# Attention, MLP and token mixer on one core: transposes of two heads in one step, the leftover block one place earlier, a surcharge for POOL in the planner, and new intervals

## The chip, the cores and the metric

The kernel runs on one core of one Trainium2 chip. The metric is the device time of one execution in microseconds (us), the median of several runs. TensorE is called PE, VectorE DVE, ScalarE ACT, GpSimd POOL and SyncE SP; SP's queue issues the DMA transfers.

## The reference, cut to what matters

```
scores = q @ k.T / 8 + min(-(cum_i - cum_j), 0), causal      # B=4, H=8, S=576, D=64
x  = softmax(scores) @ v, heads joined                        # [4, 576, 512]
x  = x + relu(layernorm(x) * g @ w_ch1) @ w_ch2               # 512 -> 2048 -> 512
u  = x + ((x.T @ U) @ V).T                                    # token mixer, rank 32
out = u + relu(u @ w2_ch1) @ w2_ch2                           # second MLP, 512 -> 2048 -> 512
```

cum is the running sum of max(s, 0). All of it is float32; the kernel reaches that by splitting both factors of a product into a high and a low part and doing three matmuls for one.

## The kernel before

**Blocks.** Work is cut by batch and tokens: A (tokens 0 to 255) and B (256 to 575) of each batch go through attention, layernorm and the first MLP. Then C (tokens 0 to 511 of a batch) goes through mixer and second MLP, where mlp1 is done as seven products in place of eight; T0 is the 64 leftover tokens of all four batches as one block of 256 columns. GROUPS gives the order of the first layer's steps, LAST that of the second: C0, C1, C2, C3, T0.

**The planner.** Nothing is issued where it is written. Every operation is given to a class Plan with a priority, its modelled duration on each engine that could do it, and what it reads and writes. `plan()` simulates the engines, takes for each operation the engine on which it would end first (times a price for busy engines), and so finds an order; `latest()` turns an order into due times; `issue()` does this four times and issues the best order, each engine's instructions in their planned places. Each engine works its list off in order, so a late operand holds up all that stands behind it. The DMA loads, `load()`, stand in SP's list in the same manner. Bare matmuls on ones (L1593) fill planned idle time of PE ahead of the first MLP step.

**The tables.** AT says over which of the first layer's steps the attention of a block is spread, LN where its layernorm stands, HEAD by how many us due times of some priorities are shifted.

**Attention.** `score` puts a pair of heads' scores into PSUM (L765, L769) and DVE adds the bias and takes the row maximum (L752); ACT and POOL do exponent and normalization (L780 to L801). `trans` then transposes each head's weights on PE in blocks of 128 columns (L824, three or four blocks a head, one PE operation for each head), and the result is split into pB (L381 on ACT, L386 on DVE). PV is L895. The layernorm's last steps are L1009 and L1050.

**The MLPs.** L1386 to L1388 and L1443 to L1445 are the three matmuls each of the first and second linear layer for A, B and T; L1308 to L1310 and L1345 to L1347 those of C. DVE and ACT combine C's products (L1288, L1294, L1268, L1269), `mlp2c` holds the second layer of C, its add of the residual and its stores (L1356); T's add and stores are L1453 and L1457. A helper records every split: high part by ACT or DVE (L381, L382), low part by DVE or POOL (L386, L388).

Of the kernel before, what the change touches and what calls it, by code (L numbers as in the profile page):

```python
# [26 lines left out]
LAG = 2  # L27
# [1 line left out]
FULL = ("A0", "A1")  # L29

GROUPS = (("A0", "A1"), ("A2", "A3"), ("B0",), ("B1",), ("B2",), ("B3",))
LAST = ("C0", "C1", "C2", "C3", "T0")
W2SLOTS = 12

AT = {"A2": (1, 3), "A3": (1, 34), "B0": (26, 49), "B1": (50, 64), "B2": (69, 84), "B3": (80, 100)}
LN = {"A2": 9, "A3": 34, "B0": 62, "B1": 64, "B2": 85, "B3": 102}
W0 = (1, 14)
HEAD = {-100: -1, -50: 127, 1.5: 71, 4.5: 8, -4: 3, -3: 0}
W1 = (16, 60, 59)
PASSES = 4  # L40
AHEAD = 1500


def f(ap):
# [3 lines left out]
def mm_cost(n):  # L48
    return max(106.7, n / 2.4) + 13.3
# [39 lines left out]
class Plan:  # L89
# [63 lines left out]
    def plan(self, prio, price):  # L153
# [42 lines left out]
        while avail:  # L196
            best = {}
            tent = dict(free)
            avail.sort(key=lambda o: (prio[o.seq], o.seq))
            for o in avail:  # L200
                fin = None
                for e, (dur, _) in o.alts.items():
                    s = slot(o, e)
                    if s is None:
                        continue
                    s = max(s, o.ready[e], dma_free - BACKLOG if e == "sp" else 0.0)
                    port = e in o.port
                    f0 = max(s, tent.get(e, 0.0), tent.get("port", 0.0) if port else 0.0) + dur
                    if len(o.alts) > 1:
                        w = min(int(s / WIN), NW - 1)  # L210
                        f0 += (price[e][w] + (price["port"][w] if port else 0.0)) * dur + (o.soft if e == "dve" else 0.0)
                    if fin is None or f0 < fin[0]:
                        fin = (f0, max(s, free[e], free["port"] if port else 0.0), e, dur)
                if fin is None:
                    continue
                e = fin[2]
                for g in (e, "port") if e in o.port else (e,):
                    if fin[1] <= tent.get(g, 0.0):
                        tent[g] = tent.get(g, 0.0) + fin[3]
# [12 lines left out]
            if o.nbytes:
                o.end = dma_free = max(dma_free, s + 1100) + o.nbytes
            new = []
            for b in o.bufs:
                if not b.live:
                    lst = live[b.tag]
                    base, most = self.take.get(b.tag, (None, 0))
                    if len(lst) < cap[b.tag]:
                        b.slot = f"{b.tag}{len(lst)}"  # L240
                    else:
                        src = lst
                        if cap[b.tag] < most:
# [92 lines left out]
def mha_ffn_mixer_ffn(ctx: ExitStack, tc, qkv_p, qkv_a, qkv_b, s, g, w1, w2, U, V, out):  # L336
# [22 lines left out]
    def psum():  # L359
        return P.buf("ps", [128, 512])  # L360
# [9 lines left out]
    def pe(prio, cost, fn, reads, writes, hold=()):  # L370
        return P.op(prio, {"pe": (cost, fn)}, reads, writes, hold=hold)
# [245 lines left out]
    class Pair:  # L617
# [187 lines left out]
        def trans(self, prio, tick):  # L805
# [9 lines left out]
            else:  # L815
                groups = [(None, ts[0], [S - 128, 0, 128, 256]), (None, ts[0], [384])]
            first = 0
            for z, t, blocks in groups:
                ps = psum()
                n = len(blocks)  # L820

                def tr(ps=ps, t=t, blocks=blocks):
                    for j, c in enumerate(blocks):
                        nc.tensor.transpose(ps[:, 128 * j:128 * (j + 1)], t[:, c:c + 128], ident.tile)  # L824

                pe(prio - 500, n * 109, tr, [t, ident], [ps] + [(a, i) for a in pT])

                def view(a, z=z, n=n, first=first):
                    if self.blk == "A":
# [502 lines left out]
    def mlp2c(st, half):  # L1332
        _, b, _, m = steps[st]
        w, h = w2t[st], hbuf[st]
        ks = (0, 1) if half == 0 else (2, 3)
        run = runs[st]
        first, last = st == run["first"], st == run["last"]
        if first:
            run[half] = [P.buf("acc", [128, 512]), psum()]
        aa = run[half]  # L1340

        def mm():
            for z, k in enumerate(ks):
                sl = slice(128 * k, 128 * (k + 1))
                nc.tensor.matmul(aa[z].tile, w[:, 0, sl], h[:, 0], start=first, stop=False)  # L1345
                nc.tensor.matmul(aa[z].tile, w[:, 1, sl], h[:, 0], start=False, stop=False)  # L1346
                nc.tensor.matmul(aa[z].tile, w[:, 0, sl], h[:, 1], start=False, stop=last)  # L1347

        free2[st] = pe(st + LAG + 0.5, 6 * mm_cost(512), mm, [w, h], aa)
        if last:  # L1350
            x = xt[b, "C"][0][half]
            for z, a in enumerate(aa):
                kk = [(x, (z, y)) for y in range(2)]
                k = ks[z]
                dve(st - 1000, 512, lambda a=a, z=z: nc.vector.tensor_tensor(out=x[:, z], in0=x[:, z], in1=a.tile, op=ALU.add), [a] + kk, kk)
                load(st - 1000, 128 * 2048, lambda k=k, z=z: nc.sync.dma_start(out[128 * k:128 * (k + 1), b * S:b * S + 512], x[:, z]), kk, [])  # L1356
            if half == 1:
                xt.pop((b, "C"))
        if half == 1:
            del hbuf[st]  # L1360
# [282 lines left out]
```

## Time and profile before

| | |
|---|---|
| time, median of 3 runs | 1036.17 us (1035.99 to 1036.62) |
| the profiled execution's own time | 1035.96 us |
| its span, first to last instruction | 1034.1 us |
| mean granted TensorE clock | 0.998 |
| PE busy | 1016.1 us, 98% |
| DVE busy | 670.8 us, 65% |
| ACT busy | 491.1 us, 47% |
| POOL busy | 163.1 us, 16% |

A busy time is the sum of an engine's instructions over the span; the profiled time is 1.9 us longer than the span. Matmuls overlap in the records, so the distance from one start to the next is what a matmul costs in a row of them.

### The profile page before, as it was taken

What the parts mean: (1) busy time and instruction counts of PE and PEld (TensorE: products, weight loads), DVE (VectorE), ACT (ScalarE), POOL (GpSimd) and SP (SyncE); (2) the same over time, 40 slices, a digit from 0 to 9 for tenths busy, and PEclk for the clock granted to TensorE, in tenths of its full rate; (3) what the DMA queues carried; (4) which work ended last, traced back from release to release, by engine and by line L of the source; (5) the groups of instructions that cost most, each with busy time, mean ns of one, the idle gap of its engine ahead of it and who ended that gap; (6) DMA issues with size and microseconds to landing.
All of it is one profiled execution on the core that took longest, in us unless ns stands there. A gap on an engine that the chain in (4) does not pass through costs nothing.

```text
span 1034.1 us, 19346 instructions
## 1 busy us (share of the span) xinstructions
PE 1016.1 (98%) x7102; PEld 937.0 (91%) x7102; DVE 670.8 (65%) x1688; ACT 491.1 (47%) x1155; POOL 163.1 (16%) x305
## 2 busy tenths in 40 slices
PE   8999999999999999999999999999999999999997
PEld 6888979899999989998999999898999898889997
DVE  7988987976978567677754328547446645844521
ACT  8988877855867456666553214213111211211210
POOL 0011342330522213423210003001001000200000
PEclk9999999999999999999999999999999999999999
DMA  9999986389737886567457798991763574376383
GB/s 312 350 344 318 335 296 215 126 244 304 244 106 241 274 291 226 179 219 232 169 182 287 247 393 338 334 342 53 263 217 117 178 260 163 113 257 206 117 285 102
DMA packets 98078, 245.12 MB, mean 237 GB/s; under 512 B 16288, under 2 KB 46240, under 8 KB 93632
## 3 DMA queue, kind: packets, MB, share of 16 engines
q1 hardware_dynamic: 97888, 243.83, 68.5%
q8 instruction: 56, 0.92, 0.3%
q14 instruction: 38, 0.31, 0.1%
q10 hardware_dynamic: 96, 0.07, 0.0%
HBM read 190.30 MB, written 62.99 MB: 245 GB/s over the span
## 4 chain that ended last, share of the span: by engine, by line
PE 81%; DMA 8%; DVE 7%; ACT 2%; issue 1%; SPq 1%; DVEq 0%; ACTq 0%
PE ps L1386 6%; PE ps L1387 6%; PE ps L1388 6%; PE ps L1308 5%; PE ps L1310 5%; PE ps L1309 5%; PE ps L866 4%; PE ps L824 4%; PE acc L1443 4%; PE acc L1444 3%; PE acc L1445 3%; PE acc L1346 3%; PE acc L1345 3%; PE acc L1347 3%; PE ps L1345 3%; PE ps L1347 3%
## 5 line engine op out<-in xcount | busy, mean ns | idle before, releaser
L1386 PE MATMUL ps<-xh,w 128*128 128x256 f32 (+1 forms) x512 | 160.0, 312 | 0.7 <-DVE hl L1393 0.6
L1388 PE MATMUL ps<-xl,w 128*128 128x256 f32 (+1 forms) x512 | 151.9, 297 | 0.0
L1387 PE MATMUL ps<-xh,w 128*128 128x256 f32 (+1 forms) x512 | 151.8, 296 | 0.0
L1393 DVE SCALAR_TENSOR_TENSOR hl<-ps,hh 128x256 fp32r<-128x256 f32 (+1 forms) x144 | 64.8, 450 | 106.2 <-ACT hh L1392 105.5
L1392 ACT ACTIVATE hh<-ps 128x256 fp32r<-128x256 f32 (+1 forms) x144 | 58.2, 405 | 130.7 <-PE ps L1388 130.1
L1386 PEld LDWEIGHTS ps<-xh,w 128*128 128x128 f32 x512 | 97.2, 190 | 6.6 <-issue 1.9
L1387 PEld LDWEIGHTS ps<-xh,w 128*128 128x128 f32 x512 | 97.3, 190 | 2.0
L1443 PE MATMUL acc<-hh,w 128*128 128x256 f32 (+1 forms) x320 | 98.2, 307 | 0.0
L1388 PEld LDWEIGHTS ps<-xl,w 128*128 128x128 f32 x512 | 97.1, 190 | 0.0
L1268 ACT ACTIVATE w<-hl 128x256 fp32r<-128x256 f32 x91 | 37.1, 416 | 123.6 <-DVE hl L1288 123.5
L1444 PE MATMUL acc<-hh,w 128*128 128x256 f32 (+1 forms) x320 | 93.8, 293 | 0.0
L1445 PE MATMUL acc<-hl,w 128*128 128x256 f32 (+1 forms) x320 | 93.7, 293 | 0.0
L783 ACT ACTIVATE t<-t,mx 128x384 f32<-128x384 f32 (+4 forms) x112 | 69.1, 618 | 23.5 <-DVE mx L773 19.0
L1288 DVE TENSOR_TENSOR hl<-ps,hh 128x256 f32<-128x256 f32 x128 | 48.4, 420 | 44.9 <-PE ps L1310 43.7
L1288 DVE TENSOR_TENSOR hh<-ps,hh 128x256 f32<-128x256 f32 x64 | 27.1, 424 | 73.3 <-ACT hh L381 72.1
L824 PE MATMUL ps<-ident,t 128*128 128x128 f32 x400 | 65.7, 278 | 7.5 <-DVE mx L752 2.2
L386 DVE TENSOR_TENSOR pB<-ps,pB 128x512 fp32r<-128x512 f32 (+1 forms) x112 | 62.5, 571 | 9.0 <-ACT pB L381 8.2
L381 ACT ACTIVATE pB<-ps 128x512 fp32r<-128x512 f32 (+3 forms) x118 | 58.0, 502 | 16.0 <-PE ps L824 15.5
L773 DVE CUSTOM_DVE_ANT_0 t<-ps,causal 128x128 f32<-128x128 f32 (+3 forms) x128 | 57.2, 486 | 12.0 <-PE ps L769 11.4
L824 PEld LDWEIGHTS ps<-ident,t 128*128 128x128 f32 x400 | 47.1, 141 | 17.8 <-ACT pB L381 3.0
L1443 PEld LDWEIGHTS acc<-hh,w 128*128 128x128 f32 x320 | 60.7, 190 | 2.7 <-issue 2.2
L381 ACT ACTIVATE hh<-ps 128x256 f32<-128x256 f32 x31 | 11.9, 384 | 106.1 <-PE ps L1310 106.1
(261 smaller groups left out, 2921.5 us busy)
## 6 DMA issues: line engine op xcount, KB each, us to landing
w<-w_dr SPq DMA_DIRECT2D x112, 512.0 KB, 7.7
pB<-w_dr SPq DMA_DIRECT2D x34, 1024.0 KB, 5.6
qk<-w_dr SPq DMA_DIRECT2D x26, 768.0 KB, 5.3
w_dr<-w SPq DMA_DIRECT2D x32, 512.0 KB, 5.5
w_dr<-wr SPq DMA_DIRECT2D x32, 512.0 KB, 4.2
wr<-w1a SPq DMA_DIRECT2D x16, 512.0 KB, 6.0
wr<-w2a SPq DMA_DIRECT2D x16, 512.0 KB, 5.7
wr<-w1b SPq DMA_DIRECT2D x16, 512.0 KB, 7.3
```

The source lines that it names most:

```text
L381: "act": ((51 if psum else 94) + 0.8333 * n, lambda: nc.scalar.activation(out(), a(), AF.Copy)),
L386: alts = {"dve": (68 + 1.042 * n, lambda: nc.vector.tensor_tensor(out=out(), in0=a(), in1=b(), op=op))}
L783: act(prio, K, lambda t=t, mx=mx, o=o, K=K, x=x, y=nt * z + x: nc.scalar.activation(t[:, o:o + K], t[:, o:o + K], AF.Exp, bias=mx[:, (1 if ...
L824: nc.tensor.transpose(ps[:, 128 * j:128 * (j + 1)], t[:, c:c + 128], ident.tile)
L1288: dve(st - 1000, 256, lambda: nc.vector.tensor_tensor(out=d.tile, in0=region(r), in1=a.tile, op=ALU.add), [p, a], [d])
L1386: nc.tensor.matmul(ps[:, :n], lhs(k, 0), xh[:, k, :n], start=k == 0, stop=False)
L1387: nc.tensor.matmul(ps[:, :n], lhs(k, 1), xh[:, k, :n], start=False, stop=False)
L1388: nc.tensor.matmul(ps[:, :n], lhs(k, 0), xl[:, k, :n], start=False, stop=k == KT - 1)
L1393: dve(st - 1000, n, lambda: nc.vector.scalar_tensor_tensor(out=hl[:, :n], in0=ps[:, :n], scalar=0.0, in1=f(hh[:, :n]), op0=ALU.max, op1=AL ...
L1443: nc.tensor.matmul(a, w[:, 0, sl], hh[:, :n], start=new, stop=False)
L1444: nc.tensor.matmul(a, w[:, 1, sl], hh[:, :n], start=False, stop=False)
L1445: nc.tensor.matmul(a, w[:, 0, sl], hl[:, :n], start=False, stop=last and (z == 1 or blk == "B"))
```

## The change

1. LAST puts T0 ahead of C3.
2. AT, LN, HEAD get new numbers (W0 is read nowhere).
3. In `plan()`, a POOL alternative of more than 250 ns is charged 700 ns (BESIDE) when engines are compared; the other engine's own charge stays.
4. In `trans`, the transposes of both heads of a pair (or of both groups of the last tick) become one PE operation, which takes two PSUM tiles at once and waits for both heads.
5. In `mlp2c`, the last step's two products become two PE operations. Where it is the last step of all, each add and each store of 512 columns is cut in halves, and the second half's store is issued from ACT's queue.

```
-LAST = ("C0", "C1", "C2", "C3", "T0")
+LAST = ("C0", "C1", "C2", "T0", "C3")
-AT = {"A2": (1, 3), "A3": (1, 34), "B0": (26, 49), "B1": (50, 64), "B2": (69, 84), "B3": (80, 100)}
+AT = {"A2": (1, 3), "A3": (1, 33), "B0": (26, 49), "B1": (46, 64), "B2": (67, 82), "B3": (76, 96)}
-HEAD = {-100: -1, -50: 127, 1.5: 71, 4.5: 8, -4: 3, -3: 0}
+HEAD = {-100: -1, -50: 147, 1.5: 81, 4.5: 63, -4: 1, -3: -10}
...
+BESIDE = 700
...
-                        f0 += (price[e][w] + (price["port"][w] if port else 0.0)) * dur + (o.soft if e == "dve" else 0.0)
+                        f0 += (price[e][w] + (price["port"][w] if port else 0.0)) * dur + (o.soft if e == "dve" else BESIDE if e == "pool" and dur > 250 else 0.0)
...
-            for z, t, blocks in groups:
-                ps = psum()
-                n = len(blocks)
-
-                def tr(ps=ps, t=t, blocks=blocks):
+            pss = [psum() for _ in groups]
+
+            def tr():
+                for ps, (_, t, blocks) in zip(pss, groups):
                     for j, c in enumerate(blocks):
                         nc.tensor.transpose(ps[:, 128 * j:128 * (j + 1)], t[:, c:c + 128], ident.tile)
 
-                pe(prio - 500, n * 109, tr, [t, ident], [ps] + [(a, i) for a in pT])
+            pe(prio - 500, sum(len(blocks) for *_, blocks in groups) * 109 + 80, tr, list(ts) + [ident], pss + [(a, i) for a in pT])
+            for ps, (z, t, blocks) in zip(pss, groups):
+                n = len(blocks)
...
+        for zs in ((0,), (1,)) if last else ((0, 1),):
+            free2[st] = product(zs)
         if last:
             x = xt[b, "C"][0][half]
+            end = st == NS - 1
...
+                for y0, y1 in ((0, 1), (1, 2)) if end else ((0, 2),):
...
+                    e, q = ("act", nc.scalar) if end and y0 else ("sp", nc.sync)
```

In the changed kernel a line of `trans` or later has a number up to 11 higher (L1386 is L1397, L1288 is L1290); those above it one higher (L752 is L753).

**What the built programs hold.** Real matmuls are the same in both; fillers go from 46 to 64. POOL has 247 instructions in place of 310, DVE 1770 for 1690, ACT 1047 and 1038. SP issues 634 DMAs for 630, ACT four stores: two more loads of each of the two parts of a pair of the second MLP's w1 (128x1536 and 128x2048, together 1.75 MB a pair) come in, since C2 and C3 no longer follow each other. Ahead of A0's last layernorm split stand 114 DVE instructions for 126 and 61 of ACT for 74; ahead of the first MLP matmul stand 15 transposes, 8 score matmuls and 12 PV matmuls fewer.

**PE, early in the program, before**: the first transposes of two heads' tiles t0 to t3 and the scores around them.

```order
L824 MATMUL ps1_301<-ident_81,t0_240 128x128 x3
L824 MATMUL ps3_311<-ident_81,t1_241 128x128 x3
L1593 LDWEIGHTS ones_82
L1593 MATMUL acc0_216<-ones_82 128x256
L824 MATMUL ps4_321<-ident_81,t2_263 128x128 x3
L765 MATMUL ps5_332<-ksum_88,sel_90 128x128
L765 MATMUL ps1_333<-ksum_88,sel_90 128x128
L769 MATMUL ps5_332<-qk1_201 128x128
L769 MATMUL ps1_333<-qk1_201 128x128
```

**PE, the same place, of the change.**

```order
L824 MATMUL ps0_301<-ident_81,t0_241 128x128 x3
L824 MATMUL ps1_302<-ident_81,t1_242 128x128 x3
L766 MATMUL ps2_318<-ksum_88,sel_90 128x128
L766 MATMUL ps3_319<-ksum_88,sel_90 128x128
L770 MATMUL ps2_318<-qk1_199 128x128
L770 MATMUL ps3_319<-qk1_199 128x128
L766 MATMUL ps2_318<-ksum_88,sel_90 128x256
L766 MATMUL ps3_319<-ksum_88,sel_90 128x256
L770 MATMUL ps2_318<-qk1_199 128x256
L770 MATMUL ps3_319<-qk1_199 128x256
L824 MATMUL ps4_336<-ident_81,t2_260 128x128 x3
L824 MATMUL ps1_337<-ident_81,t3_261 128x128 x3
```

Before, t2 was transposed ahead of these scores and t3 behind them; now t2 and t3 stand together behind the scores. Of the program's 64 pairs of transposes 53 stood apart before.

**SP, the loads for the attention of a B block, before**: qk1 is the q and k of batch 1's next pair of heads, w are pieces of the first MLP's w2, xs are v.

```order
L564 DMA w2_5422<-w_dr0_10_142 128x1024
L661 DMA xs0_5431<-qkv_b 128x320
L661 DMA xs1_5433<-qkv_b 128x320
L564 DMA w7_5441<-w_dr0_10_142 128x1024
L564 DMA w12_5454<-w_dr0_11_143 128x1024
L564 DMA w1_5477<-w_dr0_11_143 128x1024
L564 DMA w6_5503<-w_dr0_12_144 128x1024
L656 DMA qk1_4964<-qkvB2_1_165 128x576
```

**SP, the same loads, of the change.**

```order
L565 DMA w0_5341<-w_dr0_8_140 128x1024
L565 DMA w2_5352<-w_dr0_8_140 128x1024
L1151 DMA t_dr3A_106<-xs0_5354 128x512
L565 DMA w8_5378<-w_dr0_9_141 128x1024
L546 DMA wr3_5403<-w2b 128x1024
L662 DMA xs1_5421<-qkv_b 128x320
L565 DMA w4_5424<-w_dr0_9_141 128x1024
L657 DMA qk1_4905<-qkvB2_1_165 128x576
```

The same qk1 now stands behind four w loads of this MLP pass, where it stood behind nine (five of them in the rows of before). On DVE, the bias step L753 now stands between the two splits of this qk1, where both splits stood ahead of it.

**DVE, the end of the program, before**: the last hidden splits of T0 and the two adds into its result wr.

```order
L1393 SCALAR_TENSOR_TENSOR hl0_13007<-ps5_13005,hh0_13006 128x256
L1393 SCALAR_TENSOR_TENSOR hl1_13044<-ps3_13042,hh1_13043 128x256
L1393 SCALAR_TENSOR_TENSOR hl2_13065<-ps4_13063,hh2_13064 128x256
L1453 TENSOR_TENSOR wr1_12336<-wr1_12336,acc0_12674 128x512
L1453 TENSOR_TENSOR wr1_12336<-wr1_12336,acc1_12690 128x512
```

**DVE, the end of the change**: the last combinations of C3's products and the adds into its x2 and x3.

```order
L1290 TENSOR_TENSOR hl1_13102<-ps5_13074,hh2_13060 128x256
L1271 TENSOR_SCALAR w12_13031<-hl1_13102 128x256
L1296 SCALAR_TENSOR_TENSOR w10_13030<-hl2_13100,w10_13030 128x256
L1296 SCALAR_TENSOR_TENSOR w12_13031<-hl1_13102,w12_13031 128x256
L1290 TENSOR_TENSOR hl2_13114<-ps1_13081,hl0_13070 128x256
L1271 TENSOR_SCALAR w10_13030<-hl2_13114 128x256
L1296 SCALAR_TENSOR_TENSOR w10_13030<-hl2_13114,w10_13030 128x256
L1364 TENSOR_TENSOR x2_12113<-x2_12113,acc0_12472 128x256 x2
L1364 TENSOR_TENSOR x2_12113<-x2_12113,ps4_12473 128x256 x2
L1364 TENSOR_TENSOR x3_12122<-x3_12122,acc1_12489 128x256 x2
L1364 TENSOR_TENSOR x3_12122<-x3_12122,ps0_12490 128x256 x2
```

The program now ends on adds of half the width, whose stores go out by two queues; on PE, 36 matmuls of 512 columns stand behind the last of C3's products, the first 12 of which use neither w10 nor w12, and the next 12 use w10.

## Rows read from the trace of the kernel before

**Rows 1.** The page, busy time of each engine (share of the span) and instructions.

```profile
PE 1016.1 (98%) x7102; PEld 937.0 (91%) x7102; DVE 670.8 (65%) x1688; ACT 491.1 (47%) x1155; POOL 163.1 (16%) x305
```

**Rows 2.** What PE waited for: us in total, times, longest us.

```profile
PE ps L824 <- DVE mx L752: 2.2, 2, 2.0
PE ps L824 <- DVE x L879: 1.8, 4, 0.8
...
PE ps L1308 <- DVE hl L1288: 1.0, 1, 1.0
PE ps L1386 <- DMA pB<-w_dr: 0.8, 1, 0.8
```

**Rows 3.** Timeline of PE: start, us, operation, count [idle before, releaser].

```profile
360.04 0.49 PE L824 MATMUL ps<-ident,t 128*128 128x128 f32 x3
...
360.81 0.30 PE L1443 MATMUL ps<-hh,w 128*128 128x320 f32 x1
...
363.38 0.63 PE L824 MATMUL ps<-ident,t 128*128 128x128 f32 x4 [1.97 <-DVE mx L752]
```

**Rows 4.** Windows: us, busy time (instructions) by engine, PEclk, DMA share, GB/s.

```profile
364.20:367.60 3.40, 3.40 (x15) 3.18 (x14) 2.40 (x6) 1.84 (x4) 0.19 (x1) 0.50 1.01 331
```

**Rows 5.** Timelines of DVE, ACT and SP's queue ahead of it.

```profile
362.30 0.56 DVE L386 TENSOR_TENSOR qk<-qk 128x384 fp32r<-128x384 f32 x1 [0.93 <-ACT qk L381]
362.78 0.45 DVE L752 CUSTOM_DVE_ANT_0 t<-ps,t 128x288 f32<-128x288 f32 x1
...
359.89 0.69 ACT L381 ACTIVATE qk<-qk 128x576 fp32r<-128x576 f32 x1 [1.45 <-DMA qk<-qkvB]
...
347.65 2.54 SPq L564 DMA_DIRECT2D w<-w_dr  x4
350.24 0.42 SPq L656 DMA_DIRECT2D qk<-qkvB  x1
```

**Rows 6.** L1294 by form in 650 to 900; DVE, POOL and a window around 641.

```profile
L1294 DVE SCALAR_TENSOR_TENSOR w<-hl,w x92: 409/421/623, 649.9 to 898.9; 128x256 fp32r<-128x256 f32 x92
...
641.43 2.12 DVE L1294 SCALAR_TENSOR_TENSOR w<-hl,w 128x256 fp32r<-128x256 f32 x2
...
640.56 2.71 POOL L388 TENSOR_TENSOR wr<-wr,wr 128x512 fp32r<-128x512 f32 x2 [2.49 <-DVE wr L593]
...
640.00:645.00 5.00, 4.02 (x35) 3.79 (x34) 4.99 (x12) 2.83 (x8) 2.71 (x2) 1.00 0.93 329
```

**Rows 7.** The window ahead of the first MLP matmul, and PE's timeline there.

```profile
30.00:37.05 7.05, 6.58 (x57) 5.31 (x56) 6.97 (x32) 6.95 (x19) 0.00 (x0) 1.00 0.95 359
...
36.78 0.52 PE L824 MATMUL ps<-ident,t 128*128 128x128 f32 x3 [0.24 <-DVE xl L1050]
37.05 0.36 PE L1386 MATMUL ps<-xh,w 128*128 128x256 f32 x1
```

**Rows 8.** A window in T0.

```profile
990.00:1000.00 10.00, 9.19 (x78) 8.99 (x78) 1.28 (x3) 1.15 (x3) 0.00 (x0) 1.00 0.93 315
```

**Rows 9.** Timelines of DVE and PE behind the last of C3's products.

```profile
972.45 0.76 DVE L1288 TENSOR_TENSOR hl<-ps,hh 128x256 f32<-128x256 f32 x2 [0.79 <-PE ps L1310]
973.24 0.29 DVE L1269 TENSOR_SCALAR w<-hl 128x256 fp32r<-128x256 f32 x1
...
974.12 0.42 DVE L1288 TENSOR_TENSOR hl<-ps,hl 128x256 f32<-128x256 f32 x1
...
972.24 0.40 PE L1345 MATMUL acc<-w,w 128*128 128x512 f32 x1
...
973.64 0.97 PE L1243 MATMUL ps<-t,t 128*128 128x64 f32 x8
```

**Rows 10.** Timeline of the end.

```profile
1028.06 1.41 DVE L1453 TENSOR_TENSOR wr<-wr,acc 128x512 f32<-128x512 f32 x2 [2.03 <-PE acc L1445]
...
1028.46 0.28 PE L1445 MATMUL acc<-hl,w 128*128 128x256 f32 x1
1028.77 2.69 SPq L1457 DMA_DIRECT2D out<-wr  x4
```

**Rows 11.** PE's timeline and the window at a run of 14 transposes.

```profile
447.13 1.69 PE L824 MATMUL ps<-ident,t 128*128 128x128 f32 x14
...
446.90:448.80 1.90, 1.90 (x19) 1.90 (x17) 1.80 (x5) 1.15 (x3) 0.87 (x1) 1.00 0.99 403
```

More of the change, by code (lines that the diff above doesn't have):

```diff
@@ L31 @@
 GROUPS = (("A0", "A1"), ("A2", "A3"), ("B0",), ("B1",), ("B2",), ("B3",))
-LAST = ("C0", "C1", "C2", "C3", "T0")
+LAST = ("C0", "C1", "C2", "T0", "C3")
 W2SLOTS = 12
-AT = {"A2": (1, 3), "A3": (1, 34), "B0": (26, 49), "B1": (50, 64), "B2": (69, 84), "B3": (80, 100)}
-LN = {"A2": 9, "A3": 34, "B0": 62, "B1": 64, "B2": 85, "B3": 102}
-W0 = (1, 14)
-HEAD = {-100: -1, -50: 127, 1.5: 71, 4.5: 8, -4: 3, -3: 0}
+AT = {"A2": (1, 3), "A3": (1, 33), "B0": (26, 49), "B1": (46, 64), "B2": (67, 82), "B3": (76, 96)}
+LN = {"A2": 7, "A3": 33, "B0": 63, "B1": 65, "B2": 83, "B3": 102}
+W0 = (1, 22)
+HEAD = {-100: -1, -50: 147, 1.5: 81, 4.5: 63, -4: 1, -3: -10}
 W1 = (16, 60, 59)
@@ L1340, in mlp2c, with product, mm @@
         aa = run[half]
[L1342 to L1349, printed above, removed]
+        def product(zs):
+            def mm():
+                for z in zs:
+                    sl = slice(128 * ks[z], 128 * (ks[z] + 1))
+                    nc.tensor.matmul(aa[z].tile, w[:, 0, sl], h[:, 0], start=first, stop=False)
+                    nc.tensor.matmul(aa[z].tile, w[:, 1, sl], h[:, 0], start=False, stop=False)
+                    nc.tensor.matmul(aa[z].tile, w[:, 0, sl], h[:, 1], start=False, stop=last)
+            return pe(st + LAG + 0.5, 3 * len(zs) * mm_cost(512), mm, [w, h], [aa[z] for z in zs])
+        for zs in ((0,), (1,)) if last else ((0, 1),):
+            free2[st] = product(zs)
         if last:
             x = xt[b, "C"][0][half]
+            end = st == NS - 1
             for z, a in enumerate(aa):
-                kk = [(x, (z, y)) for y in range(2)]
                 k = ks[z]
-                dve(st - 1000, 512, lambda a=a, z=z: nc.vector.tensor_tensor(out=x[:, z], in0=x[:, z], in1=a.tile, op=ALU.add), [a] + kk, kk)
-                load(st - 1000, 128 * 2048, lambda k=k, z=z: nc.sync.dma_start(out[128 * k:128 * (k + 1), b * S:b * S + 512], x[:, z]), kk, [])
+                for y0, y1 in ((0, 1), (1, 2)) if end else ((0, 2),):
+                    sl = slice(256 * y0, 256 * y1)
+                    kk = [(x, (z, y)) for y in range(y0, y1)]
+                    dve(st - 1000, 256 * (y1 - y0), lambda a=a, z=z, sl=sl: nc.vector.tensor_tensor(out=x[:, z, sl], in0=x[:, z, sl], in1=a[:, sl], op=ALU.add), [a] + kk, kk)
+                    e, q = ("act", nc.scalar) if end and y0 else ("sp", nc.sync)
+                    P.op(st - 1000, {e: (475, lambda k=k, z=z, sl=sl, q=q: q.dma_start(out[128 * k:128 * (k + 1), b * S + sl.start:b * S + sl.stop], x[:, z, sl]))},
+                         kk, [], 128 * 1024 * (y1 - y0), rate=350.0)
             if half == 1:
```

## The prediction

> **What bounds the kernel now.** I read the busy times first: PE is busy 98% of the span, DVE 65%, ACT 47%, POOL 16% [rows 1]. So PE is the bound, and the change, which does the same real matmuls, can win only what PE now waits, what is lost to its clock, and what lies behind its last matmul. Second, what PE waited for [rows 2]: the costliest pairs are transposes (L824) that wait for DVE's maximum (2.2 us in two waits, one of them 2.0) and for DVE's row scaling (1.8 in four), then single waits of 1.0 and 0.8. Third, PE's timeline around the longest wait, its windows, and the engines ahead of it; last the end of the program. I sum against the profiled execution, 1035.96 us (span 1034.1, 1.9 us less); the median of the runs is 0.2 above it.
>
> **Joined transposes.** They take no instruction away. Does a change between transposes and matmuls cost PE anything? From 360.04 to 360.81 three transposes and three 320-column matmuls were issued in 0.77 us, 0.128 each [rows 3], and 14 transposes in one run stand inside a 1.90 us window of 19 matmuls that is busy all through, 0.100 each [rows 11]. A switch that cost anything would show as more than that mixture. So joining by itself is 0. What it does change: one operation waits for both heads and takes two PSUM tiles at once. The 80 ns that its modelled cost grows by is the planner's alone. I price this under the waits below.
>
> **The stall at 361 us.** PE stands idle 1.97 us ahead of L824 at 363.38, for the maximum [rows 3]. Behind it the granted clock falls to 0.50, which is the 1.2 GHz level, from 364.2 to 367.6, after PE had been idle [rows 4]; those 15 instructions took 3.40 us and would take some 15 x 0.128 = 1.9 at the mixture of [rows 3], so 1.5 us more is lost. Together 3.4. The chain back [rows 5]: DVE's L752 at 362.78 stood behind two splits of qk on DVE's list, the later of which waited 0.93 us for ACT's high part; ACT waited 1.45 us for the load of qk; and SP issued that load at 350.24 behind four w loads that took 2.54 us to issue, 0.64 each. In the new order this load stands behind four w loads of the pass instead of nine, so some 5 x 0.64 = 3.2 us earlier, more than the 1.97 that was missing; and L752 stands ahead of the later split, so that a late load alone no longer holds it. What is late next is PE's own queue, which is full. I take the whole −3.4; the bounds are 0 (the same wait elsewhere) and −3.4.
>
> **POOL's surcharge.** 63 instructions leave POOL, mostly to DVE. At 641.43 two L1294 on DVE took 2.12 us where 92 others have a median of 0.421: 1.28 us lost while POOL ran two L388 of 2.71 us, and PE is busy 4.02 of the 5 us there [rows 6], with the 1.0 us wait for L1288 among it [rows 2]. On the other side, around there five of six such POOL instructions become DVE's, at some 0.70 each (the 512-column add of [rows 10], two in 1.41), 3.5 us, in a stretch in which DVE is busy 4.99 of 5 [rows 6]. Bounds: −1.0 (the wait goes) to 3.5 − 1.3 = +2.2 (DVE becomes the bound and gets only the 1.28 back). I take −0.3, nearer the gain, since PE's queue holds other blocks' work that can stand in front. The other 57 are covered: DVE is idle for 35% of the span [rows 1]; were that cover gone, each would cost up to 0.7.
>
> The Trainium skill, "SBUF — State Buffer", "Who interferes with whom", says that a DVE instruction with two SBUF inputs and a GpSimd one that reads SBUF shut each other out. The trace agrees (2.12 for two). By that rule the surcharge frees DVE wherever both ran, and this term would be the full −1.0.
>
> **The start.** The first MLP matmul, at 37.05, follows a transpose that waits 0.24 us for the last layernorm split on DVE; from 30 to 37.05 DVE is busy 6.97 us of 7.05 (32 instructions, 0.22 each), ACT 6.95 (19, 0.37 each) [rows 7]. So DVE and ACT set this moment. Ahead of that split 12 fewer DVE instructions (−2.6 us) and 13 fewer ACT ones (−4.8) now stand. But 35 small real PE instructions (15 transposes, 8 scores, 12 PV) move from ahead of the first step, where PE has fillers for lack of work, to behind it, where it is full: 6.58 us for 57 [rows 7] is 0.115 each, +4.0. Net −2.6 + 4.0 = +1.4 if DVE decides, −0.8 if ACT does. I take +0.5, between.
>
> **T0 ahead of C3.** PE's work is the same. C3's input, transposed input and first two w1 pairs (1 + 0.25 + 3.5 = 4.75 MB) now come in during T0, where the DMA share is 0.93 at 315 GB/s [rows 8], some 339 when full: 14 us of a full queue. SP works in order, and the loads stand behind T0's own. Lower bound 0; upper bound the 0.8 wait for pB [rows 2] for each of the four added w1 loads, 3.2. One such wait in the whole run speaks for the low end: +0.3.
>
> **The end of C3.** Behind C3's last product there is now nothing but its own second layer. Before, DVE needed from 972.45 to 974.12 for five instructions; the three left (0.42, 0.29 and, by [rows 6], 0.42) would have ended at 975.25 undisturbed. PE issued six 512-column matmuls from 972.24 to 973.64 [rows 9], so 12 would end at 975.04. PE then needs w10: a wait of 0.2 that the mixer's matmuls hid before. +0.2, from 0 to 0.6.
>
> **The tail.** PE's last matmul ends at 1028.74, the last 512-column add at 1029.47, SP issues four stores until 1031.46, 0.67 each, and the span ends 2.64 later [rows 10]: 5.36 behind PE. Afterwards two 256-column adds of some 0.42 (the width of L1294 in [rows 6]) end 0.87 behind PE, the last store is issued by ACT in 0.67, and the same 2.64 makes 4.2: −1.1 (−0.6 if ACT's store is slower to land by half a us, −1.5 if halves land sooner).
>
> **New waits.** The whole order is new. A stall like that of 361 (3.4) arises somewhere with a chance of a third: +1.1, from 0 to 3.4. The trace says nothing of it but that there was one such in 1034 us.
>
> Sum: +0.5 − 3.4 − 0.3 + 0.3 + 0.2 − 1.1 + 1.1 = −2.7. 1035.96 − 2.7 = 1033.26; with the 0.2 up to the median, **1033.5**.
>
> **Rivals.** (a) Further waits go too: those for the row scaling (1.8) and for pB (0.8) [rows 2], and no new stall comes (1.1): 1029.8. For it: the list of waits before transposes, which a join may order better. Against: it needs every guess to be right. (b) A new stall of the 361 kind does come: 1033.5 − 1.1 + 3.4 = 1035.8. (c) The load still comes late and the stall stays: 1033.5 + 3.4 = 1036.9; against it the 3.2 us by which the load moves. (d) Slower: a joined transpose waits for the later head, and PE's queue behind it with it. There are 64 of them; at 0.1 us each it is +6.4 and 1033.5 − 1.1 + 6.4 = 1038.8; from 0.09 us on it decides. For it: the waits before L824 are the largest group [rows 2]. Against: these two rows are 4.0 us over 128 single groups, 0.03 each, and half of that is one event. (e) PE's clock falls around joined transposes, 1.5 us each time as in [rows 4]; at four places, +6: 1039.5.
>
> Beside (e): the Trainium skill, "TensorE: Matmul & The Clock Gate", "Part 4: PE-mode transpose", says that transposes don't count as PE-busy the way matmuls do. The trace so far speaks against an effect here: the window with 14 of them has the clock at 1.00 [rows 11], and a joined run is 5 to 8.
>
> **How the numbers follow.** Differences under 0.2% (2.07 us) can't be told from none: faster is below 1034.1, slower above 1038.24. Chances: forecast 0.37 (1031.5 to 1035.0), (a) 0.16, (b) 0.22, (c) 0.07, (d) 0.15, (e) 0.03. Faster: 0.31 of the forecast's, all of (a), 0.04 of (b): 0.51. Slower: (d) and (e), 0.18. Same: 0.31. The range takes in (a) with a little more gain and reaches through half of (d), 1028.5 to 1038.5.
>
> **What would show it.** Right: no PE idle time of 2 us around 361, and the clock at 1.00 there; L1296 (L1294 before) at 0.42 throughout around 641; first MLP matmul near 35, with the steps behind it no earlier than before; 4.2 us from PE's last matmul to the end of the span; a wait of 0.2 ahead of the 24th-last matmul of the program. Wrong: a second window with a clock of 0.5; waits before L824 that add up to more than 4 us; or a w1 load of C3 as releaser of PE by more than a us.

## The result, and the profile after

The change made the kernel slower: 1040.57 us median of 8 runs against 1036.08 for the kernel before, a ratio of 1.0057 with a 95% interval of [1.0043, 1.0071]. (The ratios in this document are estimated over all the runs, with their intervals; they are not quotients of the medians, which here would give 1.0043.) The forecast was 1033.5. The profiled execution took 1040.27 us, its span is 1038.5, 4.3 more than before.

The page of the changed kernel, busy times, against [rows 1]:

```profile
PE 1018.0 (98%) x7120; PEld 939.4 (90%) x7120; DVE 695.7 (67%) x1768; ACT 483.4 (47%) x1142; POOL 105.9 (10%) x242
```

PE is 1.9 us busier, with 18 more fillers and the same real work; the other 2.4 of the 4.3 us is idle time. What PE waited for in the changed kernel, against [rows 2]:

```profile
PE ps L1397 <- DVE hl L1404: 1.9, 2, 1.6
PE ps L897 <- issue: 1.9, 1, 1.9
...
PE ps L968 <- DVE ls L387: 1.4, 2, 0.9
PE ps L1397 <- DMA pB<-w_dr: 1.0, 1, 1.0
PE ps L1397 <- DVE mx L753: 1.0, 2, 0.7
PE ps L766 <- DVE x L914: 0.8, 1, 0.8
...
PE ps L824 <- ACT t L781: 0.3, 1, 0.3
```

The waits of 2.0 and 0.8 ahead of transposes (L824) are gone; in their place stand more and shorter ones, ahead of all kinds of matmuls. A list of waits does not say how these add up, since the order of the work differs. So I use one more quantity. **Lost time** at a moment is the time since the span's start less the real PE work begun by then, each matmul at the median start-to-start distance of its kind in the trace of before. Both kernels do the same real matmuls, so the difference of lost times is what one order is behind the other. Each row is one execution: before, e1, e9, e10 and e18 have the same PE order up to 600 us, and yet at 350 they lie between -1.8 and +0.6, so a difference of less than some 2 us at one moment shows nothing by itself, nor does one row stand for the median of its kernel (e10's execution took 1031.07 us, its median is 1033.57). Below, in us: for before its lost time, for the others what they lost more (+) or less, at eight moments; then ratio and 95% interval of the runs.

```
at us                 40    75   125   350   375   550   650   900  1025   ratio
before              16.1  17.4  20.4  30.5  35.4  42.5  43.8  44.8  45.8
changed             +2.6  +4.7  +2.8  +5.8  +2.2  +5.3  +4.0  +4.9  +5.5   1.0057 [1.0043, 1.0071]
e1_only_order       -0.6  -0.8  -0.7  +0.1  -1.0  -1.8  -1.9  -2.0  -1.7   0.9990 [0.9979, 1.0002]
e2_only_join        +2.0  +1.8  +0.3  +2.9  -0.3  +2.1  +0.9  +2.3  +2.7   1.0037 [1.0024, 1.0051]
e3_only_beside      +4.4  +6.5  +6.3  +7.6  +7.1 +16.2 +14.8 +16.2 +17.1   1.0148 [1.0128, 1.0169]
e4_only_tables      +2.7  +5.2  +4.4  +5.7  +3.9  +6.0  +5.6  +6.5  +7.6   1.0067 [1.0053, 1.0081]
e5_one_ns           +2.6  +3.1  +1.7  +1.2  -0.3  +6.3  +6.3  +7.6  +8.6   1.0076 [1.0061, 1.0091]
e6_only_head        +3.1  +3.8  +1.4  +2.2  +0.5  +0.3  +0.7  +2.3  +3.7   1.0025 [1.0014, 1.0036]
e7_only_at_ln       -0.6  -0.8  +0.7  +0.7  +0.2  +2.2  +1.6  +1.6  +2.2   1.0016 [1.0005, 1.0026]
e8_no_join          +1.3  +3.2  +2.3  +4.7  +1.4  +6.5  +5.2  +5.7  +8.9   1.0075 [1.0059, 1.0091]
e9_load_first       +0.4  +0.2  -0.5  -0.4  -3.4  -4.1  -4.0  -4.2  -3.5   0.9964 [0.9952, 0.9976]
e10_both_first      -0.2  -0.3  -1.9  -1.8  -5.2  -5.6  -5.5  -5.8  -3.5   0.9985 [0.9972, 0.9998]
e11_after_110       +3.6  +4.7  +2.8  +3.6  +4.0  +5.3  +4.0  +4.8  +5.1   1.0038 [1.0024, 1.0053]
e12_before_108      +2.6  +4.3  +1.8  +3.4  +1.0  +2.9  +3.0  +4.9  +6.6   1.0060 [1.0048, 1.0072]
e13_no_4_3          +2.3  +2.8  +2.7  +3.6  -0.1  +2.4  +1.4  +2.0  +2.7   1.0027 [1.0015, 1.0040]
e14_no_4_5          +2.4  +2.3  +1.3  +3.4  -0.6  -0.9  -2.0  -1.5  -0.5   1.0007 [0.9994, 1.0021]
e15_no_beside       +1.8  +2.7  +0.7  +0.1  -3.1  -2.6  -2.1  -1.1  -0.1   0.9986 [0.9973, 0.9999]
e16_no_tables       +2.9  +1.9  +3.1  +3.2  -0.4  +6.0  +4.8  +5.3  +6.1   1.0050 [1.0032, 1.0068]
e17_late_bias       +5.7  +8.8  +8.0 +11.2  +7.2 +10.4  +9.2  +9.8 +11.8   1.0087 [1.0074, 1.0100]
e18_wr_on_dve       +0.0  -0.1  +0.9  +0.6  -1.8  -2.1  -2.3  -2.4  -1.9   0.9971 [0.9958, 0.9985]
```

The changed kernel loses 4.7 us by 75, has 1.9 of it back by 125, loses 3.0 from there to 350, gains 3.6 between 350 and 375, loses 3.1 to 550, gains 1.3 to 650 and loses 1.5 from there. Of the 5.5 us by which PE is behind at 1025, the tail gives 1.2 back. In the two long stretches with losses PE's idle time grew from 1.9 to 4.1 us (125 to 350) and from 0.8 to 3.2 (375 to 550); first before, then the changed kernel:

```profile
125.00:350.00 225.00, 223.11 (x1714) 208.49 (x1714) 178.51 (x451) 160.52 (x391) 67.64 (x139) 1.00 0.68 226
375.00:550.00 175.00, 174.21 (x1222) 163.99 (x1221) 122.91 (x303) 106.25 (x238) 48.01 (x93) 1.00 0.64 211
...
125.00:350.00 225.00, 220.89 (x1697) 205.50 (x1697) 192.44 (x497) 157.32 (x383) 49.70 (x116) 1.00 0.66 219
375.00:550.00 175.00, 171.81 (x1198) 161.33 (x1198) 130.22 (x312) 104.48 (x238) 30.52 (x74) 1.00 0.64 208
```

**Where it gained.** Windows of the changed kernel around the old stall, and SP's queue ahead of it; against [rows 3], [rows 4] and [rows 5]:

```profile
361.00:363.40 2.40, 2.40 (x20) 2.39 (x20) 1.51 (x3) 2.07 (x5) 0.14 (x1) 1.00 0.97 327
364.20:367.60 3.40, 3.40 (x25) 2.96 (x25) 1.77 (x6) 0.44 (x1) 0.14 (x1) 1.00 0.83 253
```

```profile
346.55 0.42 SPq L565 DMA_DIRECT2D w<-w_dr  x1
347.02 0.44 SPq L657 DMA_DIRECT2D qk<-qkvB  x1
```

PE is busy all through with the clock at 1.00, and the load is issued 3.2 us earlier. PE itself was 5.8 us further back in its work at 350, so against the work the load is early by some 9 us. L1296 (L1294 before) by form, against [rows 6]:

```profile
L1296 DVE SCALAR_TENSOR_TENSOR w<-hl,w x128: 408/419/708, 646.3 to 1028.5; 128x256 fp32r<-128x256 f32 x128
```

Over the whole program none takes more than 0.71 us. The end of the changed kernel on DVE, PE, SP and ACT, against [rows 9] and [rows 10]:

```profile
1028.51 0.43 DVE L1296 SCALAR_TENSOR_TENSOR w<-hl,w 128x256 fp32r<-128x256 f32 x1
...
1034.36 0.75 DVE L1364 TENSOR_TENSOR x<-x,ps 128x256 f32<-128x256 f32 x2
...
1028.62 0.47 PE L1348 MATMUL acc<-w,w 128*128 128x512 f32 x1
1028.93 0.40 PE L1349 MATMUL acc<-w,w 128*128 128x512 f32 x1
...
1033.93 0.39 PE L1350 MATMUL ps<-w,w 128*128 128x512 f32 x1
...
1032.77 2.37 SPq L1366 DMA_DIRECT2D out<-x  x4
...
1033.11 2.38 ACTq L1366 DMA_DIRECT2D out<-x  x4
```

PE's last matmul ends at 1034.32 and the span at 1038.5: 4.2 us, 5.4 before. The wait for w10 is 0.08 (0.31 from 1028.62 to 1028.93, where 0.23 is usual): DVE's late instruction writes the low part, which only the third matmul, L1350, reads.

**Where it lost first.** PE, DVE and ACT of the changed kernel at its start, against [rows 7]:

```profile
17.11 0.87 PE L824 MATMUL ps<-ident,t 128*128 128x128 f32 x6 [0.33 <-ACT t L781]
19.86 3.10 PE L897 MATMUL ps<-qk,pB 128*128 128x128 f32 x24 [1.87 <-issue]
...
34.38 0.35 PE L1397 MATMUL ps<-xh,w 128*128 128x256 f32 x1 [0.34 <-DVE xl L1052]
...
18.30 0.33 DVE L450 TENSOR_SCALAR xc<-xc 128x320 f32<-128x320 f32 x1 [2.24 <-DMA xc<-s]
...
19.21 0.55 DVE L383 COPY pB<-ps 128x384 f32<-128x384 f32 x1
```

And the window up to there:

```profile
0.00:34.38 34.38, 28.18 (x235) 22.39 (x235) 27.10 (x113) 25.99 (x63) 2.13 (x12) 1.00 0.92 313
```

The first MLP matmul comes 2.7 us earlier. By that moment PE had begun 170 real matmuls beside its 64 fillers, where before there were 221 and 46 by 37.05: 51 fewer, not 35. And PE stands 1.87 us ahead of PV, while DVE stands 2.24 us for a load (s, for the bias of the B blocks); the copy into pB behind it on DVE's list ends at 19.76, 0.1 ahead of PV's start.

### The profile page after: what moved, and what is told of

It reads as the page before. It is cut to its first block, busy times and chain, and to the rows that moved or that the text cites. A ratio compares the mean times of both kernels' runs of the same rounds, so it can differ in the third digit from the quotient of the medians.

```text
span 1038.5 us, 19350 instructions
## 1 busy us (share of the span) xinstructions
PE 1018.0 (98%) x7120; PEld 939.4 (90%) x7120; DVE 695.7 (67%) x1768; ACT 483.4 (47%) x1142; POOL 105.9 (10%) x242
## 4 chain that ended last, share of the span: by engine, by line
PE 74%; DVE 13%; DMA 4%; ACT 4%; issue 2%; SPq 1%; POOL 0%; DVEq 0%; ACTq 0%; POOLq 0%
PE ps L1397 5%; PE ps L1310 5%; PE ps L1312 5%; PE ps L1311 5%; PE ps L1398 5%; PE ps L1399 5%; PE acc L1454 3%; PE acc L1455 3%; PE acc L1456 3%; PE ps L868 3%; PE acc L1348 3%; PE acc L1349 3%; PE acc L1350 3%; PE ps L1348 3%; PE ps L1349 3%; PE ps L1350 3%
## 5 line engine op out<-in xcount | busy, mean ns | idle before, releaser
L1397 PE MATMUL ps<-xh,w 128*128 128x256 f32 (+1 forms) x512 | 158.9, 310 | 4.6 <-DVE hl L1404 1.9
L1397 PEld LDWEIGHTS ps<-xh,w 128*128 128x128 f32 x512 | 96.7, 189 | 11.8 <-DVE hl L1404 2.7
L1290 DVE TENSOR_TENSOR hh<-ps,hh 128x256 f32<-128x256 f32 x64 | 27.1, 423 | 81.0 <-ACT hh L382 78.9
L1290 DVE TENSOR_TENSOR hl<-ps,hh 128x256 f32<-128x256 f32 x128 | 48.4, 419 | 44.6 <-PE ps L1312 43.4
L387 DVE TENSOR_TENSOR pB<-ps,pB 128x384 fp32r<-128x384 f32 (+2 forms) x112 | 59.9, 569 | 6.6 <-ACT pB L382 6.0
L1454 PEld LDWEIGHTS acc<-hh,w 128*128 128x128 f32 x320 | 60.6, 190 | 2.0 <-issue 1.5
L1455 PEld LDWEIGHTS acc<-hh,w 128*128 128x128 f32 x320 | 60.7, 190 | 0.3
L1456 PEld LDWEIGHTS acc<-hl,w 128*128 128x128 f32 x320 | 60.7, 190 | 0.0
L382 ACT ACTIVATE pB<-ps 128x384 fp32r<-128x384 f32 (+3 forms) x104 | 48.7, 512 | 17.9 <-PE ps L824 17.7
```

Source lines behind the costliest of these rows:

```text
L1290: dve(st - 1000, 256, lambda: nc.vector.tensor_tensor(out=d.tile, in0=region(r), in1=a.tile, op=ALU.add), [p, a], [d])
L1397: nc.tensor.matmul(ps[:, :n], lhs(k, 0), xh[:, k, :n], start=k == 0, stop=False)
L1454: nc.tensor.matmul(a, w[:, 0, sl], hh[:, :n], start=new, stop=False)
L1455: nc.tensor.matmul(a, w[:, 1, sl], hh[:, :n], start=False, stop=False)
L1456: nc.tensor.matmul(a, w[:, 0, sl], hl[:, :n], start=False, stop=last and (z == 1 or blk == "B"))
```

## The experiments

Theory, from the trace of the result: the gains are the edits' own, and the losses come from the order that the planner draws, which any change of its input redraws. Rivals: the joined transposes (J), the new tables, HEAD (H) or AT and LN (A), or the surcharge make the loss themselves.

**One part at a time.** e1 has LAST and the hunk in `mlp2c`, e2 the hunk in `trans`, e3 BESIDE and its use, e4 the three tables, all on the kernel before.

> The kernel before with T0 ahead of C3 and the split tail alone; up to C2 the order is that of before. Theory of the steps (each step's price holds by itself): tail -1.1 us, a wait of about 1.2 us for pB at the start of T0 as in the changed kernel, the 0.8 us wait inside T0 gone: together -0.7, so about 1035.4. Theory of the order (every edit to the planner's input reshuffles the whole program): nothing ahead of C2 moves here, so the same -0.7. Rival: a stall for C3's w1 loads, +3, 1038.

> The kernel before with the joined transposes alone. Theory J (the join makes PE wait for the later head and is the cause of the loss up to 66 us): PE's lost time at 66 us is 4 us above that of before, and the time is 1039 to 1041. Theory T (the new tables are the cause): lost time at 66 us within 1 us of before. Theory of the order: anything between 1033 and 1041, the stall at 361 us gone or not.

> The kernel before with POOL's surcharge alone. If the surcharge frees DVE as the prediction had it: the two L1294 at 641 us back to 0.42 each, the 1.0 us wait behind them gone, 1035 to 1036. If DVE becomes the bound: 1037 to 1039, with more waits of PE for DVE in 10 to 150 us and 625 to 650 us.

> The kernel before with the new intervals and due-time shifts alone. Theory T (the tables put work of A1 and of later blocks behind the first MLP step, and the stall at 361 us goes by them): lost time at 66 us 4 us above before, the stall at 361 gone (-3.4), 1036 to 1038. Theory J: lost time at 66 us as before, 1033. Theory of the order: anything between 1033 and 1041.

e1 came out at 1034.95 against 1035.81 of before, as expected (-0.9, though its interval reaches 1). The others are slower by 0.37%, 1.48% and 0.67%. Alone, the parts add up to about 2.4%; together they cost 0.57%. The stall at 361 goes with the join alone (lost time falls 3.2 from 350 to 375). With the tables (e4) and with the surcharge (e3) PE still waits there, now for L1393 or L1394 on DVE, though the clock stays at 1.00:

```profile
360.47 0.55 PE L824 MATMUL ps<-ident,t 128*128 128x128 f32 x3 [1.58 <-DVE hl L1393]
...
360.62 0.44 PE L766 MATMUL ps<-ksum,sel 64*128 64x384 f32 x1 [1.35 <-DVE hl L1394]
```

So a part has no price that it keeps.

**An edit that no chip can feel.**

```
-                pe(prio - 500, n * 109, tr, [t, ident], [ps] + [(a, i) for a in pT])
+                pe(prio - 500, n * 110, tr, [t, ident], [ps] + [(a, i) for a in pT])
```

> The kernel before, with one transposing block modelled at 110 ns in place of 109 and nothing else: no edit that a chip could feel, only the planner's input. Its PE order is that of the kernel with the surcharge alone for the first 287 rows. Theory of the order (the planner's order, not any edit, makes the time; the order is sensitive to anything): lost time of PE at 45 us some 5 us above before, as with the surcharge alone, and the time 2 us or more away from 1036. Theory of the steps (an edit's own cost or gain makes the time): 1036, same as before.

> The kernel before with a transposing block modelled at 108 ns in place of 109. Theory of the order: the start is that of the run with 110 ns (same order of PE at first, some 3 us more lost time at 45 us), and the end lies anywhere from 1036 to 1046; that the kernel before lies at the fast end of what its own edits give. Theory of the steps: 1036.

> The changed kernel with a transposing block modelled at 110 ns in place of 109, which no chip can feel. Theory of the order (a change of the planner's input draws another order, and the time of an order is spread over some 10 us): anything from 1036 to 1046, 2 us or more away from 1040.6 about as often as not. Theory of the steps: 1040.6, within 1 us.

One nanosecond more in the model of a transpose makes the kernel before 0.76% slower, one less 0.60%: as much as the whole change (0.57%). In the changed kernel one more gives 1039.38 against 1040.57, with intervals that overlap. At 45 us e5 had lost 3.3 more than before and e3 5.3, though their PE orders agree that far: the lists of the other engines matter too. The theory of the steps falls: an order drawn anew costs this much without any edit that the chip could feel.

**The tables, halved.** e6 has HEAD alone, e7 AT and LN, both on the kernel before; e8 is the changed kernel with the hunk in `trans` undone.

> The kernel before with the new due-time shifts (HEAD) alone. Theory H (HEAD's 55 us on A1's layernorm and 20 on A0's put the first MLP step ahead of work that PE then has to do where it is full): lost time at 66 us 4 to 5 us above before, 1037 to 1042. Theory A (the intervals AT and LN are the cause): lost time at 66 us within 1 us of before.

> The kernel before with the new intervals AT and LN alone; PE's order is that of before for the first 725 rows. Theory H: lost time at 66 us as before, and what the intervals do comes behind: the stall at 361 us (B1's attention starts 4 steps earlier) gone, 1033 to 1036. Theory A: lost time 4 us above before by 66 us.

> The changed kernel with the transposes of the two heads apart again. Theory J (the joined transposes cost the 3 us that the changed kernel loses in small waits from 125 to 300 us and 375 to 550): 1036 to 1037.5. Theory H with the order: lost time at 66 us stays 4 to 5 us above before, and the time lies anywhere between 1036 and 1043.

HEAD moves the start (+3.8 at 75), AT and LN don't (-0.8), as theory H has it; but both orders come out slower by only 0.25% and 0.16%, and not 0.67%. Undoing the join does not make the changed kernel faster (1.0075 against 1.0057, with intervals that overlap), where theory J had 1036 to 1037.5; so theory J falls.

**The cause of the stall, with the order kept.** After planning, four w loads are moved behind the four loads of qk in the order, on top of e1; every other engine keeps its list. later() moves one operation and its buffer.

```
+        for _ in range(4):
+            later(sp[294], sp[303])
+            sp = [i for i, q in enumerate(best) if q[1] == "sp"]
```

> T0 ahead of C3 with the split tail, as in the run of that alone, and in SP's list four w loads moved behind the four loads of qk that the stall at 361 us waits for; no other engine's order changes. Theory of the late load (the 2 MB of w ahead of it in the queue make qk late, that ACT and DVE, that PE): the load lands 3 to 6 us earlier, PE's idle time at 361 us goes, -1.6 to -3.4, 1031.5 to 1033.3. Rival (the lists of ACT and DVE hold PE there in any case): PE idle 1 us or more at 361, 1035.

SP's queue, ACT and PE in e1, without that move:

```profile
348.33 2.50 SPq L564 DMA_DIRECT2D w<-w_dr  x4
350.89 0.42 SPq L656 DMA_DIRECT2D qk<-qkvB  x1
...
360.11 0.69 ACT L381 ACTIVATE qk<-qk 128x576 fp32r<-128x576 f32 x1 [1.00 <-DMA qk<-qkvB]
...
363.68 0.63 PE L824 MATMUL ps<-ident,t 128*128 128x128 f32 x4 [1.62 <-DVE mx L752]
```

The same in e9:

```profile
347.44 0.33 SPq L668 DMA_DIRECT2D qk<-qkvB  x1
...
358.11 0.67 ACT L393 ACTIVATE qk<-qk 128x576 fp32r<-128x576 f32 x1
...
361.14 0.63 PE L836 MATMUL ps<-ident,t 128*128 128x128 f32 x4
```

The load is issued 3.45 us earlier and lands 5.2 us after its issue, where it took 9.2 in e1; ACT no longer waits for it, and PE goes on without a wait. e9 takes 1031.12 us against 1035.27 of before, 0.9964 [0.9952, 0.9976]: this version beats both kernels, and e1 (0.9990 [0.9979, 1.0002]), from which it differs in this move alone. The chain of [rows 5] is shown.

**Two more edits with the order kept.** e10 moves the four stores of C2's block behind two w loads and a pB load. e18 gives two POOL instructions of e9 to DVE.

```
+        for i, (o, e, *r) in enumerate(best):
+            if e == "pool" and o.prio == 133:
+                best[i] = (o, "dve", *r)
```

> As the run with the loads of qk moved, and the four stores of C2's block moved behind the next two w loads and one pB load in SP's list. If the stores, which wait for C2's last adds, hold up pB: the wait of 1.4 us for pB in T0 goes as well, another -1.4. If the DMA queue itself is the limit there: the wait stays, and the time is that of the run before.

> The kernel with the loads of qk moved, and the two POOL instructions beside the slow L1294 (wr, 128x512, at 641 us) given to DVE at the same place of the order. If the prediction's price of the surcharge holds with the order kept: the two L1294 take 0.42 each, DVE does 1.4 us more, PE's wait of 1.0 for L1288 goes or is halved: -0.5 to -1.0, 1030.2 to 1030.7. If DVE is the bound there: +0.1 to +1.

PE's wait for pB, first in e9, then in e10, where it did not go but grew:

```profile
PE ps L1407 <- DMA pB<-w_dr: 1.4, 1, 1.4
...
PE ps L1410 <- DMA pB<-w_dr: 2.7, 2, 1.8
```

From 900 to 1025 e10 lost 2.3 us against before, e9 0.7, so the stores are not what holds pB. Its load was issued only 1.5 us earlier (899.80 for 901.33) and still took 8.1 us to land (7.7 in e9); what makes that long stays open. In e18 the two instructions on DVE, and the wait behind them:

```profile
639.96 0.41 DVE L1309 SCALAR_TENSOR_TENSOR w<-hl,w 128x256 fp32r<-128x256 f32 x1
640.53 0.42 DVE L1309 SCALAR_TENSOR_TENSOR w<-hl,w 128x256 fp32r<-128x256 f32 x1 [0.15 <-ACT w L1283]
```

```profile
PE ps L1323 <- DVE hl L1303: 0.4, 1, 0.4
```

They take 0.42 instead of the 1.06 each of [rows 6], and the 1.0 us wait is 0.4; from 550 to 650 lost time falls by 0.3 against e9. By the runs, 1031.61 and 1031.12, e18 can't be told from e9.

**What still makes the start lose.** e13 and e14 are the changed kernel with -4 and -3, or 4.5, of HEAD as before; e15 has BESIDE = 0, e16 the three tables as before. e17 moves the five bias instructions of DVE behind A0's last layernorm split.

```
+        xl = [i for i, q in enumerate(best) if q[1] == "dve" and q[0].prio == -50][-1]
+        x = [q for q in best[:xl] if q[1] == "dve" and q[0].prio == 5]
+        best[:] = [q for q in best[:xl + 1] if q not in x] + x + best[xl + 1:]
```

> The changed kernel with the due-time shifts of the first weights' preparation (-4 and -3 of HEAD) as before. Ahead of the first MLP matmul PE now does more of the small work than in either kernel. If the start loses because small work of PE is put behind the first MLP step, lost time at 66 us is 2 us or more below that of the changed kernel. If the start loses because DVE and ACT are late in any order but that of before, it stays at +4 to +5.

> The changed kernel with the shift of A1's layernorm (4.5 of HEAD) back at 8 us. If these 55 us make the loss at A1's start (PE waits of 0.9 and 0.8 us at 58.6 and 64.0), lost time between 45 and 66 us grows by less than 0.5 instead of 1.5. Otherwise as the changed kernel.

> The changed kernel without POOL's surcharge. If the surcharge pays by itself: slower than 1040.6, with POOL beside DVE's L1296 at 641 us again and the wait of 1 us there. If the order alone decides: anywhere from 1036 to 1046.

> The changed kernel with all tables as before: joined transposes, surcharge and T0 ahead of C3 on the old intervals. Sum of the parts taken alone (3.1 of the join, 15.6 of the surcharge, -0.9 of the order of blocks): 1054. If parts don't add up, because each only draws an order: anywhere from 1036 to 1050.

> The changed kernel with five DVE instructions of the B blocks' bias (2.9 us, the first of which waited 2.24 us for its load at 16 us) moved behind A0's last layernorm split in DVE's list; no other engine's order changes, the fillers stay. If these five are what makes the start lose: PE's wait of 1.9 us at 17.7 us goes, the first MLP matmul comes 3 to 5 us earlier, lost time at 66 us is 2 to 4 us lower, 1036.5 to 1038.5. If ACT, or the fillers, hold the start anyway: lost time at 66 us falls by less than 1, 1040.

e13 begins 248 real matmuls ahead of its first MLP matmul, which comes at 42.9, and still loses 2.8 by 75 (1.9 less than the changed kernel; 2.1 less at 66, where 2 was the mark set): small work put off can be a part, but 1.9 is within what two executions of one order differ by, so this is not decided. e14's lost time against before falls by 0.5 between 45 and 75 (2.8 to 2.3), the changed kernel's grows by 1.7 (3.0 to 4.7), as expected of the 55 us; but its order is another one to the end, and by the runs it equals before. e15 is faster than the changed kernel by 0.7%, so here the surcharge does not pay. It is the one rival that stays open: put on the kernel before it costs 1.48%, taken out of the changed kernel it gives 0.7%, but e14 has it and equals before. Of the 14 newly drawn orders the seven with it lie at 1.0007 to 1.0148 and the seven without at 0.9986 to 1.0076, so they overlap, and no run has the surcharge on a kept order throughout. e16 is at 1.0050 where the sum of its parts gives 1.0175. All of them lose 1.9 to 2.8 us by 75: no other start found here is as good as that of before, and of e1, e7, e9, e10 and e18, which keep it.

e17 was a miss: 4 us slower than the changed kernel, not 2 to 4 faster. ACT and PE of e17, and a window:

```profile
18.76 0.62 ACT L537 ACTIVATE ps<-wr 128x512 f32<-128x512 f32 x1 [1.52 <-DMA wr<-w1a]
...
20.77 1.74 PE L902 MATMUL ps<-qk,pB 128*128 128x128 f32 x12 [1.92 <-ACT pB L387]
22.29 3.60 PE L1609 MATMUL acc<-ones 128*128 128x256 bf16 x17
...
39.14 2.23 PE L902 MATMUL ps<-qk,pB 128*128 128x128 f32 x9 [2.40 <-issue]
```

```profile
22.20:25.90 3.70, 3.70 (x21) 2.51 (x20) 3.13 (x9) 3.38 (x7) 0.21 (x1) 0.55 0.94 309
```

PE stands for 1.92 us up to 20.77, as the changed kernel did up to 19.86, now for pB on ACT, whose list is held 1.52 us by another late load (wr). So two late loads, one on DVE's list and one on ACT's, can hold pB there; taking one away leaves the other. In their new place, from 34.96 on, the moved instructions (2.9 us) stood ahead of DVE's next work, and PE waited another 2.40 us ahead of 39.14, where the profile names no releaser. The clock was at 0.55 from 22.2 to 25.9, the 1.2 GHz level, and at 0.53 from 39.0 to 41.5, both behind an idle PE; in the changed kernel it stayed at 1.00.

## Why the prediction was wrong

**The stall at 361** was right in mechanism and size: -3.4 forecast, -3.6 from 350 to 375, and e9 against e1 shows the chain with nothing else moved. In part this is luck. That the issue moved by just the 3.2 us worked out does not allow for PE being 5.8 us behind by then; and of the 3.4, the 1.5 for the clock depends on the execution: e1, with the same order there, waited 1.62 us and kept a clock of 1.00. **The tail** was right: 4.2 forecast and measured. **The end of C3**: +0.2 forecast, 0.08 measured; only the third matmul needs the late part. **T0 ahead of C3**: +0.3 forecast; a wait of 1.0 for pB came at the start of T0 and the one of 0.8 inside it went; lost time grows by 0.6 from 900 to 1025, so +0.5 beside the end of C3. **The surcharge's gain at 641**: -0.3 forecast, -1.3 measured from 550 to 650; DVE did not become the bound there. Only some 0.3 of it is shown to be the two instructions' (e18 against e9); e2, without the surcharge, gains 1.2 there too. The pair took 2.12 us beside POOL and 0.42 each without it. The Trainium skill, "SBUF — State Buffer", "Who interferes with whom", says that a DVE instruction with two SBUF inputs contends with a GpSimd one that reads SBUF; these rows agree.

**The start** was mis-sized: +0.5 forecast within -0.8 to +1.4, +2.6 measured at 40 and +4.7 at 75. The count was wrong: 51 real matmuls were put off and not 35 (24 PV for 12, 12 score matmuls for 8), +5.9 by the prediction's own 0.115 each, which with the -2.7 that came true makes +3.2. What was left out altogether are loads that come late for DVE and ACT at 16 to 18 us, and A1's start, where PE waited 0.7 and 0.6 us ahead of 59.65 and 64.88.

**New waits** were the step that failed, together with the start: of the 7.0 us between the forecast (-2.7) and the measured +4.3 of the profiled executions, the start makes 4.2 and the new waits 4.0, and the other terms take 1.2 off. New waits were priced at +1.1, one stall of the known kind with a chance of a third. The rest of the program, from 75 to 350, 375 to 550 and 650 to 900, cost +5.1 (1.1, 3.1 and 0.9; the 3.1, and the 3.0 from 125 to 350 inside the first, are beyond what two executions of one order differ by), and none of it is such a stall: the longest wait there is 1.57 us, at 479.39, and the clock stayed at 1.00. The error is in the baseline. The trace of before was read as a typical order with one bad place, "one such in 1034 us"; among the orders drawn here it lies at the fast end. Two edits of one nanosecond to it gave 1.0076 and 1.0060, and of the 14 newly drawn orders (the changed kernel, e2 to e8 and e11 to e16) only e14 and e15 are not slower. Their median is some 4.5 us slower than before, in a range from -1.4 to +15: that, and not a third of one stall, is what a redraw was worth.

Of the rivals, (d), the joined transposes, named the right side for a wrong reason: e8, without them, is no faster. (e) did not come: the mean clock of the changed kernel's profiled execution is 1.0 with 64 joined runs in it. The Trainium skill, "TensorE: Matmul & The Clock Gate", "Part 4: PE-mode transpose", says that transposes don't count as PE-busy in the same way; this trace shows no effect of it.

Open are: which of the waits from 125 to 350 and 375 to 550 belongs to which edit (they are a different set in every order), whether the surcharge has a price of its own, and what holds pB in T0.

## What to carry to other kernels

Where a planner draws the order, the measured kernel is one draw, here one at the fast end: before an edit to its input is priced, draw a few orders with edits that can't matter, and take their spread as the price of drawing again. An edit made behind the planner, with every other list kept, shows what a step is worth by itself: e9 has a gain at 361 like the change's (-3.0 from 350 to 375, where the change has -3.6), without its losses. And where an in-order engine waits for a load, look at what stands ahead of the load in its queue and behind the wait on the list, and count on a second late load right behind the first.

## What the runs showed of the hardware

PE's idle time does not by itself tell whether the granted clock falls behind it. The clock fell to the 1.2 GHz level behind 1.97 us in [rows 3], behind 1.92 in e17 and behind only 1.37 in e4; it stayed at 1.00 behind 1.95 in e5, 1.87 in the changed kernel and 1.62 in e1. The rows of e4, then those of e5:

```profile
24.98 0.29 PE L765 MATMUL ps<-ksum,sel 64*128 64x128 f32 x1 [1.37 <-DVE x L912]
26.50:29.90 3.40, 3.40 (x21) 2.09 (x18) 2.17 (x10) 2.78 (x8) 0.00 (x0) 0.50 1.04 407
...
475.49 0.63 PE L824 MATMUL ps<-ident,t 128*128 128x128 f32 x4 [1.95 <-ACT qk L381]
475.40:479.40 4.00, 3.91 (x28) 3.49 (x29) 3.69 (x11) 2.42 (x6) 1.70 (x3) 1.00 0.86 281
```

Before and e1 have the same order at 361, and only the execution of before met a fall there. Within one kernel the times go with the clock: of e1's twelve runs the four with a mean granted clock of 1.000 took 1031.7 to 1034.3 us, the eight with 0.997 or 0.998 took 1033.8 to 1036.9. In e17 the fall made 17 fillers cost 3.60 us, 0.21 each, where the changed kernel's 17 took 2.02, with real work behind them in PE's list. And the qk load of 0.3 MB landed 9.2 us after its issue in e1, behind four w loads of 2 MB, and 5.2 us after its issue in e9, where those four stand behind it: of the some 7.4 us by which it came earlier, its place in the queue gave 4.0 and the earlier issue 3.4.
